# VectorE block transposes, one load of wo and a ScalarE store in a decode block with an adaptive LayerNorm

## The chip, the cores and the metric

The kernel runs on one core of one Trainium2 chip. The metric is the time of one execution on the device in microseconds (us). The profiled execution gives a span, from the first to the last instruction of the program; the run time is some 1.2 to 1.5 us longer than the span.

## The reference

One token for each of two sequences goes through a transformer block. A modulation vector is computed from `c`; attention reads a window of 1024 positions of a K and a V cache (32 heads of 192); a gated FFN follows.

```python
mod = (_silu(c) @ w_mod).reshape(c.shape[0], 6, 1, -1)
sa, ca, ga, sb, cb, gb = (mod[:, i] for i in range(6))
h = _layernorm(x) * (1 + ca) + sa            # x: [2, 1, 640]
x = x + ga * attention(h, k_cache, v_cache, wq, wo)   # wq 640 x 6144, wo 6144 x 640
h = _layernorm(x) * (1 + cb) + sb
x = x + gb * ((_gelu(h @ w_gate) * (h @ w_up)) @ w_down)  # F = 1536
```

There are two rows of activations and 76.88 MB of weights and cache, so the work is mostly to bring data in.

## The kernel before

All big operands go through one arena in SBUF. The sync engine issues the loads in a fixed order (w_mod, wq, K and V tiles, wo, gate, up, down), each as soon as the place it overwrites has been read. Small matmuls use four groups of columns of TensorE side by side, so a row of activations is kept as four pieces, on partitions 0 to 31, 32 to 63 and so on.

The normalised row `hrow` is turned to the contraction layout by matmuls with a selector (the same code serves LN1 and LN2):

```python
for j in range(KT):
    for i in range(NR):
        last = e.matmul(ps[32*i:32*i+32, BK_M, CT+2*j:CT+2*j+2], lhsT=hv[:, :, j],
                        rhs=selrow[:, i, :], ..., tile_position=(0, 32*i))
...
S.op("dve", lambda e: e.tensor_copy(out=dst_bf, in_=ps[:, BK_M, CT:CT+2*KT]...))
```

wo arrives in two loads, `WO_SPLIT = [(0, 39), (39, 9)]`; its matmuls write four partial rows, which `wo_rows` adds up. Before them, `keep_clock(9, "clock0")` runs nine filler matmuls, whose results nobody reads. Gate and up read the weights in runs of three columns:

```python
wk = wv[:, k, :].rearrange("p (m i r) -> p i m r", i=NR, r=FR)      # FR = 3
for i in range(NR):
    last = e.matmul(ps[32*i:32*i+B, bk, 0:FT]..., lhsT=h2T[:, k, :], rhs=wk[:, i, :, :], ...)
```

The gated row is turned by three matmuls and a copy (`a_T`), and w_down arrives in pieces of 8, 3 and 1 blocks, `WD_SPLIT = [(0, 8), (8, 3), (11, 1)]`. The last four matmuls, two VectorE operations and the store of 2.5 KB, issued by the sync engine, end the program.

## Time and profile before

| | before |
|---|---|
| run time, median | 185.97 us (185.87 to 185.97, 3 runs) |
| span of the profiled run | 184.9 us |
| bytes loaded | 76.88 MB, 416 GB/s over the span |
| TensorE / VectorE / ScalarE busy | 56% / 58% / 8% |
| last landing of weights / end of span | 182.05 / 184.9 us |

Busy shares say little here, since every compute engine idles much of the time.

### The profile page before, as it was taken

The page shows a single profiled execution, that of the slowest core. Times are in us where ns is not written, and L with a number is a line of the kernel's source. Part 1 is how long each engine was busy: PE and PEld are TensorE (multiplying, and loading weights), DVE is VectorE, ACT ScalarE, POOL GpSimd, SP SyncE. Part 2 cuts the span into 40 slices and gives each one's busy share as a digit, 9 for nine tenths or more (in the row PEclk, how much of TensorE's full clock was granted, in tenths as well). Part 3 has the DMA queues.
Part 4 walks back from the last instruction along what each step waited for, and adds up shares of the span by engine and source line. Part 5 has one row for each costly group of instructions (what it writes and reads, how often), then busy time and mean ns, then how long its engine had stood idle before and what let it go on. Part 6 is the DMA issues. An engine that isn't in the chain of part 4 may idle for free.

```text
span 184.9 us, 1610 instructions
## 1 busy us (share of the span) xinstructions
PE 104.3 (56%) x843; PEld 26.1 (14%) x552; DVE 106.8 (58%) x97; ACT 14.5 (8%) x28; POOL 6.7 (4%) x29
## 2 busy tenths in 40 slices
PE   0015400937666096662598667748663299866853
PEld 0011000020000000001360002400000266411211
DVE  6213000039996489965994999387995649302311
ACT  2032100060000000001000000100000100220410
POOL 7700000000000000000000000000000000000000
PEclk9999999996999759998599999987999669999999
DMA  9999998999897999999898989899999989899980
GB/s 349 433 495 425 425 425 362 429 425 495 367 511 340 511 404 447 457 394 479 374 479 365 500 351 500 383 468 436 425 450 394 491 367 486 378 388 435 419 365 28
DMA packets 2626, 76.97 MB, mean 416 GB/s; under 512 B 314, under 2 KB 444, under 8 KB 572
## 3 DMA queue, kind: packets, MB, share of 16 engines
q1 hardware_dynamic: 2604, 76.88, 96.9%
q8 instruction: 5, 0.08, 0.2%
q14 instruction: 1, 0.01, 0.0%
q10 hardware_dynamic: 16, 0.01, 0.0%
HBM read 76.88 MB, written 0.00 MB: 416 GB/s over the span
## 4 chain that ended last, share of the span: by engine, by line
DMA 57%; DVE 22%; PE 17%; ACT 1%; issue 1%; SPq 0%
DMA arena<-in_A_k_cache_dram 36%; DMA arena<-in_B_w_down_dram 14%; DVE arena L518 12%; DMA arena<-in_w_mod_dram 8%; PE ps L581 8%; DVE S_sb L537 6%; PE ps L530 5%; DVE Em L567 2%; PE ps L470 2%; DVE negm L547 1%; ACT E_sb L555 1%; PE ps L558 1%; DVE M L543 0%; PE ps L551 0%; SPq L287 0%
## 5 line engine op out<-in xcount | busy, mean ns | idle before, releaser
L530 PE MATMUL ps<-arena,ident_b 128*128 128x512 bf16 x192 | 50.7, 411 | 30.2 <-DVE arena L518 30.1
L518 DVE TENSOR_TENSOR arena<-arena,qbc 128x3072 bf16<-128x3072 bf16 x32 | 54.8, 1749 | 11.1 <-DMA arena<-in_A_k_cache_dram 11.1
L581 PE MATMUL ps<-arena,Em 128*64 128x384 bf16 x256 | 24.5, 357 | 5.6 <-DVE Em L567 5.6
L537 DVE TENSOR_REDUCE S_sb<-ps 128x32 f32<-128x1024 f32 x16 | 19.5, 1219 | 8.4 <-PE ps L530 8.4
L581 PEld LDWEIGHTS ps<-arena,Em 128*64 128x64 bf16 x256 | 15.4, 121 | 29.8 <-DVE Em L567 22.2
L567 DVE TENSOR_TENSOR Em<-E_sb,maskE 128x2048 bf16<-128x2048 bf16 x8 | 18.0, 2282 | 2.6 <-PE ps L581 2.6
L492 PE MATMUL ps<-arena,hT 128*2 128x512 bf16 x60 | 4.7, 485 | 11.7 <-DMA arena<-in_A_wq_dram 11.7
L502 DVE CAST qrow<-ps 128x512 bf16<-128x512 f32 x1 | 0.7, 693 | 15.6 <-PE ps L492 15.6
L545 PEld LDWEIGHTS ps<-ident_f,M 128*1 128x1 f32 x2 | 0.2, 80 | 61.5 <-DVE M L543 61.5
L555 ACT ACTIVATE E_sb<-S_sb,nbias 128x256 bf16<-128x256 f32 x2 | 1.0, 507 | 69.3 <-DVE nbias L553 69.3
L651 DVE COPY arena<-ps 128x320 f32<-128x320 f32 x1 | 0.5, 491 | 10.1 <-PE ps L643 10.1
L643 PE MATMUL ps<-arena,oT 128*2 128x320 bf16 x96 | 3.9, 299 | 2.4 <-DMA arena<-in_A_wo_dram 2.4
L588 ACT ACTIVATE On<-ps,rden 128x384 bf16<-128x384 f32 x2 | 1.2, 582 | 47.5 <-PE ps L581 47.5
L403 PE MATMUL ps<-ident_b,crow 2*128 2x2 bf16 x5 | 0.4, 177 | 7.9 <-POOL zsel L383 7.9
L678 PE MATMUL ps<-arena,h2T 128*2 128x384 bf16 x40 | 3.8, 455 | 1.7 <-DMA arena<-in_B_w_up_dram 1.4
L470 PE MATMUL ps<-arena,scT 128*17 128x480 bf16 x40 | 4.3, 597 | 0.5 <-DMA arena<-in_w_mod_dram 0.5
L415 PE MATMUL ps<-Em,ident_b 128*128 128x512 bf16 x17 | 4.2, 379 | 0.2 <-issue 0.2
L408 DVE CAST X<-xr 128x160 f32<-128x160 bf16 x1 | 0.2, 244 | 6.1 <-DMA xr<-in_A_x_dram 6.1
L687 DVE TENSOR_TENSOR aR<-ps,gl 128x384 bf16<-128x384 f32 x1 | 0.6, 558 | 5.4 <-PE ps L678 5.4
L424 PE MATMUL ps<-st,selstat 128*128 128x2 f32 x4 | 0.9, 298 | 4.9 <-ACT sqj L420 4.9
L478 DVE TENSOR_SCALAR opc<-modR 128x160 f32<-128x160 f32 x2 | 0.5, 245 | 5.1 <-ACT modR L475 5.1
L492 PEld LDWEIGHTS ps<-arena,hT 128*2 128x2 bf16 x20 | 0.6, 100 | 15.8 <-issue 15.8
(89 smaller groups left out, 52.6 us busy)
## 6 DMA issues: line engine op xcount, KB each, us to landing
arena<-in_A_v_cache_dram SPq DMA_DIRECT2D x4, 6144.0 KB, 27.2
arena<-in_A_k_cache_dram SPq DMA_DIRECT2D x3, 6144.0 KB, 36.0
arena<-in_A_wq_dram SPq DMA_DIRECT2D x1, 7680.0 KB, 31.3
arena<-in_A_wo_dram SPq DMA_DIRECT2D x1, 6240.0 KB, 27.0
arena<-in_A_k_cache_dram SPq DMA_DIRECT2D x2, 3072.0 KB, 42.7
arena<-in_w_mod_dram SPq DMA_DIRECT2D x1, 4800.0 KB, 14.0
arena<-in_B_w_gate_dram SPq DMA_DIRECT2D x1, 1920.0 KB, 20.7
arena<-in_B_w_up_dram SPq DMA_DIRECT2D x1, 1920.0 KB, 22.7
```

Of the source, the lines that this page charges most:

```text
L415: last = e.matmul(ps[:, BK_T, :], lhsT=ident_b[:, :], rhs=Em[:, 0, 0:512 // H, :].rearrange("p j h -> p (j h)"), start=True, stop=True)
L470: last = e.matmul(ps[32 * i:32 * i + RM, half, 0:MH].rearrange("p (m n) -> p m n", n=DR), lhsT=scT[:, k, :], rhs=wv[:, 3 * half:3 * half + ...
L492: last = e.matmul(ps[32 * i:32 * i + B, n, :], lhsT=hT[:, k, :], rhs=wv[:, kk, i, n * QW:(n + 1) * QW], start=(k == 0), stop=(k == KT - 1) ...
L518: S.op("dve", lambda e: e.tensor_tensor(out=kt, in0=kt, in1=qbc[:, b, :].unsqueeze(1).broadcast_to([P, JC, Dh]), op=ALU.mult), reads=[("qb ...
L530: last = e.matmul(o_ap, lhsT=ident_b[:, :], rhs=kt[:, :, t * GC:(t + 1) * GC], start=(t == 0), stop=(t == NCH - 1))
L537: S.op("dve", lambda e: e.tensor_reduce(out=S_sb[:, b, 2 * JC * pair:2 * JC * (pair + 1)], in_=ps[:, 2 * z:2 * z + 2, :].rearrange("p k (j ...
L547: S.op("dve", lambda e: e.tensor_reduce(out=negm[:, b, :].rearrange("p (h x) -> p h x", x=XQ), in_=ps[0:1, BK_T, 0:P].rearrange("p (h x) - ...
L555: S.op("act", lambda e: e.activation(out=E_sb[:, b, :], in_=S_sb[:, b, :], func=ACTF.Exp, scale=SCALE, bias=nbias[:, b:b + 1], accum_out=d ...
L567: S.op("dve", lambda e, z=z, j=j: e.tensor_tensor(out=Em[:, z, :, :], in0=E_sb[:, b, j:j + JE].unsqueeze(2).broadcast_to([P, JE, H]), in1= ...
L581: last = e.matmul(ps[64 * i:64 * i + 2 * H, BK_O, 0:ON], lhsT=Em[:, z, 2 * jp:2 * jp + 2, :].rearrange("p j h -> p (j h)"), rhs=view(it, l ...
L643: last = e.matmul(ps[32 * i:32 * i + B, bk, 0:w], lhsT=oT[:, t, :], rhs=wv[:, tl, lo:lo + w], start=(t < NR), stop=(t >= NT - NR), tile_po ...
L678: last = e.matmul(ps[32 * i:32 * i + B, bk, 0:FT].rearrange("p (m r) -> p m r", r=FR), lhsT=h2T[:, k, :], rhs=wk[:, i, :, :], start=(k == ...
```

## The change

The intent is to shorten the chain from the landing of wo to the end: no transposes through TensorE and PSUM, contiguous weight reads in gate and up, fewer loads, and a store issued by an engine other than the loading one. The diff, cut to its core:

```diff
-    WO_SPLIT = [(0, 39), (39, 9)]
+    WO_SPLIT = [(0, NT)]
 ...
-            S.op("pe", f, reads=["hrow", "selrow"], writes=[bank(BK_M)], name=tag + "_T")
-            S.op("dve", lambda e: e.tensor_copy(out=dst_bf[:, :, :], in_=ps[:, BK_M, ...
+            S.op("dve", lambda e: e.transpose(dst_bf[:, :, :], hrow[:, :].rearrange("p (m j) -> p j m", j=KT)),
+                 reads=["hrow"], writes=[tag + "_out"], name=tag + "_T")
 ...
-        keep_clock(9, "clock0")
+        keep_clock(31, "clock0")
 ...
-                        wk = wv[:, k, :].rearrange("p (m i r) -> p i m r", i=NR, r=FR)
-                            last = e.matmul(ps[32 * i:32 * i + B, bk, 0:FT]..., lhsT=h2T[:, k, :], rhs=wk[:, i, :, :], ...
+                            last = e.matmul(ps[32 * i:32 * i + RM, bk, 0:FT], lhsT=h2T[:, k, 0:RM], rhs=wv[:, k, i * FT:(i + 1) * FT], ...
 ...  (gelu and the product now read PSUM with a stride of 12 and write rows sorted for the transpose)
-        S.op("pe", a_T, reads=["aR", "selg"], writes=[bank(2)], name="aT_T")
-        S.op("dve", lambda e: e.tensor_copy(out=aT[:, :, 0:RM:RB]...
+        S.op("dve", lambda e: e.transpose(aT[:, :, :], aR[:, :].rearrange("p (r m) -> p r m", r=FC)), ...)
 ...
-        S.dma("sp", k_dma(out[:, 0, :]...
+        S.dma("act", k_dma(out[:, 0, :]...
```

The summing of wo in partial rows is in both kernels and its lines don't change.

More of the change, by code (lines that the diff above doesn't have):

```diff
@@ L149, in bass_adaLN_cond__sliding_block_cached__geglu_ffn__decode_kernel @@
     DD = Dh // NT
-    FR = 3
     FC = F // P
     assert B == 2 and D == KT * P and XQ * J == W and XQ * H == P and HB * NR == H and NT * P == NQ
-    assert DD * NT == Dh and DD * H == P and NR * FR == FC and FC * P == F and DR == KT * 32 and DD == XQ
+    assert DD * NT == Dh and DD * H == P and FC * P == F and DR == KT * 32 and DD == XQ
     SCALE = float(Dh) ** -0.5
@@ L203, in bass_adaLN_cond__sliding_block_cached__geglu_ffn__decode_kernel @@
         place[("wo", 0)] = (4 * HS, wo_n[0])
-        place[("wo", 1)] = (13 * HS, wo_n[1])
-        assert 4 * HS + wo_n[0] <= 9 * HS and wo_n[1] <= HS
+        assert wo_n[0] == 5 * HS
         o_g = 9 * HS
@@ L232, in bass_adaLN_cond__sliding_block_cached__geglu_ffn__decode_kernel @@
         selstat = sb("selstat", [P, P], F32)
-        selrow = sb("selrow", [P, NR, B], BF16)
         selq = sb("selq", [P, B, HB * SQW], BF16)
@@ L251, in bass_adaLN_cond__sliding_block_cached__geglu_ffn__decode_kernel @@
         hrow = sb("hrow", [P, DR], BF16)
-        hT = sb("hT", [P, KT, B], BF16)
-        h2T = sb("h2T", [P, KT, B], BF16)
+        hT = sb("hT", [P, KT, 32], BF16)
+        h2T = sb("h2T", [P, KT, 32], BF16)
         S_sb = sb("S_sb", [P, B, J], F32)
@@ L262, in bass_adaLN_cond__sliding_block_cached__geglu_ffn__decode_kernel @@
         selw = sb("selw", [P, RM], F32)
-        gl = sb("gl", [P, FT], F32)
+        assert FT <= B * J
+        gl = S_sb[:, :, :].rearrange("p b j -> p (b j)")[:, 0:FT]
         aR = sb("aR", [P, FT], BF16)
-        selg = sb("selg", [P, NR, B], BF16)
-        aT = sb("aT", [P, FC, RM], BF16)
+        aT = sb("aT", [P, FC, 32], BF16)
         fin = sb("fin", [P, DR], F32)
@@ L346, in bass_adaLN_cond__sliding_block_cached__geglu_ffn__decode_kernel @@
         S.op("pool", lambda e: e.memset(epsc[:, 1:2], EPS), reads=["epsc"], writes=["epsc"], name="epsc1")
-        for nm, t in (("scT", scT), ("aT", aT)):
+        for nm, t in (("scT", scT),):
             S.op("pool", lambda e, t=t: e.memset(t[:, :, :], 0.0), writes=[nm], name=nm + "0")
@@ L356, in bass_adaLN_cond__sliding_block_cached__geglu_ffn__decode_kernel @@
              reads=["ident_f"], writes=["ident_b"], name="ident_b")
-        S.op("pool", lambda e: e.affine_select(out=selrow[:, :, :], in_=ones_b[:, 0:1].unsqueeze(2).broadcast_to([P, NR, B]),
-                                                pattern=[[-32, NR], [-RB, B]],
-                                                compare_op=ALU.is_equal, fill=0.0, base=0, channel_multiplier=1),
-             reads=["ones_b"], writes=["selrow"], name="selrow")
-        S.op("pool", lambda e: e.affine_select(out=selg[:, :, :], in_=ones_b[:, 0:1].unsqueeze(2).broadcast_to([P, NR, B]),
-                                                pattern=[[-32, NR], [-1, B]],
-                                                compare_op=ALU.is_equal, fill=0.0, base=0, channel_multiplier=1),
-             reads=["ones_b"], writes=["selg"], name="selg")
         S.op("pool", lambda e: e.memset(selw[:, :], 0.0), writes=["selw"], name="selw0")
@@ L444, in ln_mod @@
                  reads=["lnt", "rstd", ("modR", s_idx // 3)], writes=["hrow"], name=tag + "_h")
-            def f(e):
-                last = None
-                hv = hrow[:, :].rearrange("p (m j) -> p m j", j=KT)
-                for j in range(KT):
-                    for i in range(NR):
-                        last = e.matmul(ps[32 * i:32 * i + 32, BK_M, CT + 2 * j:CT + 2 * j + 2], lhsT=hv[:, :, j], rhs=selrow[:, i, :],
-                                        start=(j == 0), stop=(j == KT - 1), skip_group_check=True, tile_position=(0, 32 * i))
-                return last
-            S.op("pe", f, reads=["hrow", "selrow"], writes=[bank(BK_M)], name=tag + "_T")
-            S.op("dve", lambda e: e.tensor_copy(out=dst_bf[:, :, :], in_=ps[:, BK_M, CT:CT + 2 * KT].rearrange("p (j b) -> p j b", b=B)),
-                 reads=[bank(BK_M)], writes=[tag + "_out"], name=tag + "_out")
+            S.op("dve", lambda e: e.transpose(dst_bf[:, :, :], hrow[:, :].rearrange("p (m j) -> p j m", j=KT)),
+                 reads=["hrow"], writes=[tag + "_out"], name=tag + "_T")
         ln_stats("ln1")
@@ L491, in f @@
                         for i in range(NR):
-                            last = e.matmul(ps[32 * i:32 * i + B, n, :], lhsT=hT[:, k, :], rhs=wv[:, kk, i, n * QW:(n + 1) * QW],
+                            last = e.matmul(ps[32 * i:32 * i + B, n, :], lhsT=hT[:, k, 0:RM:RB], rhs=wv[:, kk, i, n * QW:(n + 1) * QW],
                                             start=(k == 0), stop=(k == KT - 1), tile_position=(0, 32 * i))
@@ L675, in f @@
                     for k in range(k0, k0 + nk):
-                        wk = wv[:, k, :].rearrange("p (m i r) -> p i m r", i=NR, r=FR)
                         for i in range(NR):
-                            last = e.matmul(ps[32 * i:32 * i + B, bk, 0:FT].rearrange("p (m r) -> p m r", r=FR), lhsT=h2T[:, k, :],
-                                            rhs=wk[:, i, :, :], start=(k == 0), stop=(k == KT - 1), tile_position=(0, 32 * i))
+                            last = e.matmul(ps[32 * i:32 * i + RM, bk, 0:FT], lhsT=h2T[:, k, 0:RM], rhs=wv[:, k, i * FT:(i + 1) * FT],
+                                            start=(k == 0), stop=(k == KT - 1), tile_position=(0, 32 * i))
                     return last
@@ L683, in bass_adaLN_cond__sliding_block_cached__geglu_ffn__decode_kernel @@
         ffn_gu(0, wg_v, "gate", [(0, KT, ("wg", 0))])
-        S.op("act", lambda e: e.activation(out=gl[:, :], in_=ps[:, 0, 0:FT], func=ACTF.Gelu_apprx_tanh),
+        S.op("act", lambda e: e.activation(out=gl[:, :].rearrange("p (r m) -> p r m", r=FC), in_=ps[:, 0, 0:FT].rearrange("p (m r) -> p r m", r=FC), func=ACTF.Gelu_apprx_tanh),
              reads=[bank(0)], writes=["gl"], name="gelu")
         ffn_gu(1, wu_v, "up", [(k0, nk, ("wu", ci)) for ci, (k0, nk) in enumerate(WU_SPLIT)])
-        S.op("dve", lambda e: e.tensor_tensor(out=aR[:, :], in0=ps[:, 1, 0:FT], in1=gl[:, :], op=ALU.mult),
+        S.op("dve", lambda e: e.tensor_tensor(out=aR[:, :].rearrange("p (r m) -> p r m", r=FC), in0=ps[:, 1, 0:FT].rearrange("p (m r) -> p r m", r=FC),
+                                              in1=gl[:, :].rearrange("p (r m) -> p r m", r=FC), op=ALU.mult),
              reads=[bank(1), "gl"], writes=["aR"], name="geglu")
-        def a_T(e):
-            last = None
-            for r in range(FR):
-                last = e.matmul(ps[:, 2, NR * B * r:NR * B * (r + 1)], lhsT=aR[:, :].rearrange("p (m r) -> p m r", r=FR)[:, :, r],
-                                rhs=selg[:, :, :].rearrange("p i b -> p (i b)"), start=True, stop=True)
-            return last
-        S.op("pe", a_T, reads=["aR", "selg"], writes=[bank(2)], name="aT_T")
-        S.op("dve", lambda e: e.tensor_copy(out=aT[:, :, 0:RM:RB].rearrange("p (i r) b -> p i r b", r=FR),
-                                            in_=ps[:, 2, 0:FC * B].rearrange("p (r i b) -> p i r b", r=FR, i=NR)),
-             reads=[bank(2)], writes=["aT"], name="aT")
+        S.op("dve", lambda e: e.transpose(aT[:, :, :], aR[:, :].rearrange("p (r m) -> p r m", r=FC)), reads=["aR"], writes=["aT"], name="aT")
         for ci, (r0, nr) in enumerate(WD_SPLIT):
@@ L705, in f @@
                     for i in range(NR):
-                        last = e.matmul(ps[32 * i:32 * i + RM, BK_OT, CY:CY + DR], lhsT=aT[:, fc, :], rhs=wv[:, i, :],
+                        last = e.matmul(ps[32 * i:32 * i + RM, BK_OT, CY:CY + DR], lhsT=aT[:, fc, 0:RM], rhs=wv[:, i, :],
                                         start=(fc == WD_SPLIT[0][0]), stop=(fc == WD_SPLIT[-1][0]), tile_position=(0, 32 * i))
@@ L714, in bass_adaLN_cond__sliding_block_cached__geglu_ffn__decode_kernel @@
              reads=["fin", "X"], writes=["finb"], name="outR")
-        S.dma("sp", k_dma(out[:, 0, :].rearrange("b (i n) -> i b n", i=NR), finb[0:P:RB, :]),
+        S.dma("act", k_dma(out[:, 0, :].rearrange("b (i n) -> i b n", i=NR), finb[0:P:RB, :]),
               sem_out, reads=["finb"], name="st_out")
@@ L727, in bass_adaLN_cond__sliding_block_cached__geglu_ffn__decode_kernel @@
         body[entry:entry] = moved
-        S.emit("sp", nc.sync, tail=lambda e: e.wait_ge(sem_out, 16))
+        S.emit("sp", nc.sync)
         S.emit("pool", nc.gpsimd)
-        S.emit("act", nc.scalar)
+        S.emit("act", nc.scalar, tail=lambda e: e.wait_ge(sem_out, 16))
         S.emit("dve", nc.vector)
```

## The prediction

> **What bounds the kernel now.** I began with the page: the row of DMA activity in 40 slices, to see whether one resource is busy from end to end, and the count of moved bytes.
>
> ```profile
> DMA  9999998999897999999898989899999989899980
> ...
> HBM read 76.88 MB, written 0.00 MB: 416 GB/s over the span
> DMA 57%; DVE 22%; PE 17%; ACT 1%; issue 1%; SPq 0%
> ```
>
> The transfer engines never go quiet before the last slice, while PE and DVE are each busy under 60% of the span. So the program is a stream of 76.88 MB that begins at 0 and must end before the last weights can be used. The chain that ended last ends like this (start, duration, what):
>
> ```profile
> 155.58 26.07 DMA arena<-in_B_w_down_dram
> 181.65 0.04 issue
> 181.70 0.39 PE ps L706 x12
> 182.08 0.01 issue
> 182.09 0.28 PE ps L706 x4
> 182.37 0.02 issue
> 182.39 0.34 DVE fin L711
> 182.73 0.02 issue
> 182.75 0.33 DVE finb L713
> ```
>
> The last two pieces of the down projection wait for their weights, which land at about 181.65 and 182.08. From the last landing to the end of the 184.9 us span there are only 2.8 us: four matmuls, two VectorE operations and the store. The busy time of each engine by stretch shows how the stream ends (the columns are the stretch, its length, PE, PEld, DVE, ACT and POOL busy with counts, granted clock, DMA share, GB/s):
>
> ```profile
> 177.00:179.00 2.00, 1.55 (x20) 0.59 (x20) 0.00 (x0) 0.00 (x0) 0.00 (x0) 1.00 0.99 402
> 179.00:180.60 1.60, 0.60 (x7) 0.15 (x3) 0.76 (x2) 0.00 (x0) 0.00 (x0) 1.00 0.60 235
> 180.60:181.70 1.10, 0.74 (x33) 0.55 (x34) 0.00 (x0) 0.00 (x0) 0.00 (x0) 1.00 0.18 69
> ```
>
> All 16 transfer engines work until 179; then most are finished, and the last piece lands when the slowest one is. No compute instruction sets that moment. Finally the timeline of the part that the change touches:
>
> ```profile
> 164.80 2.89 PE L643 MATMUL ps<-arena,oT 128*2 128x320 bf16 x78 [1.78 <-DMA arena<-in_A_wo_dram]
> 168.27 0.98 PE L643 MATMUL ps<-arena,oT 128*2 128x320 bf16 x18 [0.58 <-DMA arena<-in_A_wo_dram]
> 173.45 0.37 PE L451 MATMUL ps<-selrow,hrow 128*32 128x2 bf16 x20 [0.26 <-DVE hrow L442]
> 174.09 1.91 PE L678 MATMUL ps<-arena,h2T 128*2 128x384 bf16 x20 [0.27 <-DVE h2T L455]
> 177.45 1.91 PE L678 MATMUL ps<-arena,h2T 128*2 128x384 bf16 x20 [1.45 <-DMA arena<-in_B_w_up_dram]
> 180.10 0.24 PE L693 MATMUL ps<-selg,aR 128*128 128x8 bf16 x3 [0.74 <-DVE aR L687]
> 180.65 0.73 PE L706 MATMUL ps<-arena,aT 128*17 128x160 bf16 x32 [0.31 <-DVE aT L697]
> 183.10 0.69 SPq L287 DMA_DIRECT2D out_dram<-finb  x1
> ```
>
> Here wo arrives in two parts (landing at 164.8 and 168.27), LN2 follows, gate and up run, then the first eight blocks of down. The gate matmuls wait for LN2, but the up matmuls wait for their own weights (177.45), so LN2 and gate have slack of 1.45 us today, and the down blocks then wait again for weights.
>
> **What the Trainium skill says.** (1) "VectorE: DVE Perf Modes", section "The three transpose paths": the VectorE transpose works on 32x32 blocks from SBUF to SBUF, 311 ns for 128x128 bf16. No such instruction is in this trace, so that figure is my basis. (2) "SBUF — State Buffer", section "Door 1: The DMA port swizzle", note on cachelines: a read that moves to a new 16-byte line for each access pays, with at least two accesses per line needed. The gate and up weights are read today in runs of three bf16 (6 bytes) at a pitch of 24 bytes. The trace agrees in direction: 20 gate matmuls take 1.91 us, so four side by side take 0.382 us for 384 columns, 0.99 ns a column; the wo matmuls, whose rows are contiguous, take 2.89/78 x 4 = 0.148 us for 320 columns, 0.46 ns a column. (3) "TensorE: Matmul & The Clock Gate", section "Part 1: The HAM clock gate (the "warmup" mystery)": about 3.4 us of idle halves the clock. The column of the granted clock reads 1.00 around the modulation matmuls at 14 us, yet twenty of 480 columns take 2.18 us, 0.91 ns a column after an idle time, twice wo's, so I believe the durations, not the column. It is why the filler matmuls rise from 9 to 31. (4) "DMA: Bandwidth & Descriptors", section "Issuing engines are not separate DMA queues": another issuing engine saves only the sequencer's issue time. In this trace the ACT issues of x and c took 0.61 and 0.54 us, the SP issue of the result 0.69.
>
> **The change, part by part.**
>
> LN1 transpose. Removed: 20 small matmuls (0.37 us) and a cast (0.17). Added: one VectorE transpose of 128x160, estimated at 0.311 + 32/0.96 ns = 0.34 us. The query matmuls that read it wait for wq until 32.2 us, while hT is ready at 18.7. Worth 0. The second modulation group no longer waits behind the transposes and ends some 2 us sooner, so a K load is issued at about 18.5 in place of 20.5; wq and two K tiles are queued before it, so the stream does not notice. Worth 0. The smaller GpSimd setup is done by 8.4 us anyway. Worth 0.
>
> wo in one load. The same 7680 KB are read. Its issue now also waits for the last reduction of the last K tile: 140.6 in place of 137.8 us, while the queue still holds two V tiles. Its landing stays at about 168.2, since the later part already landed last. But the 78 matmuls that ran from 164.8 now start only at 168.3, so 96 follow in a row: 96 x 0.0371 = 3.56 us, end 171.85 against 169.25. This part costs 2.6 us on the compute chain. The filler: 31 at some 0.22 us from 160.9 ends near 167.8, ahead of the landing, so it costs nothing and keeps the clock.
>
> LN2. From the end of wo to the end of hrow is 4.14 us today, unchanged: hrow ends at 171.85 + 4.14 = 176.0. Today h2T is there and gate starts 0.70 us after hrow; with a transpose of 0.34 us and its hand-over, some 0.4. Gate starts at 176.4 (today 174.09).
>
> Gate and up, read contiguously: at 0.46 ns a column, five groups of 384 take 5 x 0.178 = 0.89, with fill some 1.05 us. Gate ends 177.45, just as the up weights land (177.42); up ends 178.5, against 179.4 today. The gelu (0.49) is done at 178.0. This part gives back 0.86 us each.
>
> geglu stays near 0.56 us (reads at a pitch of 48 bytes from PSUM might add 0.1 to 0.3): 179.1. The transpose of 128x384 is 0.311 + 256/0.96 ns = 0.58 us; today three matmuls, a cast and hand-overs take 0.58 from 180.05 to 180.63. A wash. aT is ready at about 179.75, against 180.63 today.
>
> Down and end. The first eight blocks' weights land by about 180.5 (issue 155.09 + 25.4), the next at 181.65, the last at 182.08; so the gain of some 0.9 us is waited away. The operand could be as late as 181.05 (182.08 less 0.73 less 0.28) without loss. After that the four matmuls and two operations are as before, and the store's issue takes 0.6 on ACT in place of 0.69: -0.1 us. The receipt (about 1.0 us) stays.
>
> One more small term: wq, rows of 61,440 bytes like the merged wo, came in at 7.86 MB / 18.2 us = 432 GB/s, and the second wo part at 1.47 MB / 3.47 us = 425; over 18 us that is up to 0.2 us of stream, of which I count half at half belief. Sum: -0.1 - 0.05, so about 185.8 us.
>
> **The rivals.** (A) The compute chain overtakes the stream. If strided reading is not what slows gate and up, they keep 1.91 us: gate ends 178.35, up 180.25, aT is ready near 181.45, 0.4 us after the harmless limit: 186.4 us. For it: other matmuls after idle times are slow too. Against it: gate runs right after filler, up after 1.45 us of idle, and both take 1.91. If also wo ran at half clock, 3.5 us more: near 190. Against it: the filler reaches to the landing. (B) The stream itself gets shorter, by fewer and larger packets, and the slowest engine ends sooner: at most some 0.5 us, 185.3. Against it: the piece of 1280-byte rows, 160 KB, took 0.4 us, about 400 GB/s, so short rows cost little. (C) The store from ACT is slower, its queue having been unused since 2 us: up to +0.3, 186.2. For it: nothing that the profile shows.
>
> **Range and chances.** The end is tied to the landing of the last bytes, which no part moves, and the three runs of before lie within 0.1 us. B gives the low end with the store's gain, A's smaller form the high end: 185.2 to 186.4. Faster by 2% would be under 182.3 us, about where the last load lands: 1%. Slower by 2% would be over 189.7, which needs half clock and slow reads together: 1%.
>
> **What would show it.** Right: wo's 96 matmuls start at 168.3 and take about 3.6 us; gate and up take about 1.05 us each; the transposes 0.34 and 0.58 us; down's later blocks still wait for weights, landing at 181.65 and 182.08; issue on ACT near 0.6 us. Wrong: a last wait of down on aT in place of the weights, gate at 1.9 us, wo at 0.07 us or more a matmul, or a last landing moved by over 0.5 us.

## The result, and the profile after

| | before | after |
|---|---|---|
| run time, median | 185.98 us (185.87 to 186.16, 6 runs) | 186.12 us (186.03 to 186.40, 6 runs) |
| span of the profiled run | 184.9 us | 184.7 us |
| last landing of weights | 182.05 us | 181.95 us |
| instructions | 1610 | 1541 |

The ratio is 1.0008 with a 95% interval of 0.9995 to 1.0021: the same time. A ratio is the mean time of one kernel's fast runs over that of the other's of the same rounds, so it is not quite the ratio of the medians quoted. In the page of the changed kernel, the activity of the transfer engines, the bytes and the shares of the chain that ended last:

```profile
DMA  9999998999898989999898989899998999979990
...
HBM read 76.88 MB, written 0.00 MB: 416 GB/s over the span
DMA 57%; DVE 22%; PE 18%; ACT 1%; issue 1%; SPq 0%
```

The stream is as dense as before, with the same bytes. The end of the chain of waits of the changed kernel (start, duration, what):

```profile
156.83 24.71 DMA arena<-in_B_w_down_dram
181.55 0.04 issue
181.59 0.39 PE ps L676 x12
181.98 0.01 issue
181.99 0.28 PE ps L676 x4
182.27 0.02 issue
182.29 0.34 DVE fin L681
182.63 0.02 issue
182.65 0.32 DVE finb L683
```

The same waits end last: the two late pieces of w_down, now at 181.55 and about 181.95. The stretches at the end of the stream (columns as in the prediction):

```profile
179.00:180.60 1.60, 0.10 (x8) 0.13 (x12) 1.07 (x2) 0.00 (x0) 0.00 (x0) 1.00 0.59 221
180.60:181.70 1.10, 0.75 (x40) 0.54 (x40) 0.00 (x0) 0.00 (x0) 0.00 (x0) 1.00 0.15 56
```

The share of busy transfer engines falls to 0.59 and then 0.15, as before. And the timeline of the changed part:

```profile
162.39 6.64 PE L404 MATMUL ps<-Em,ident_b 128*128 128x512 bf16 x30
168.96 3.44 PE L623 MATMUL ps<-arena,oT 128*2 128x320 bf16 x96
176.60 0.35 DVE L435 STREAM_TRANSPOSE h2T<-hrow 128x160 bf16<-128x160 bf16 x1
177.01 1.80 PE L657 MATMUL ps<-arena,h2T 128*17 128x384 bf16 x40 [0.65 <-DVE h2T L435]
179.53 0.58 DVE L669 STREAM_TRANSPOSE aT<-aR 128x384 bf16<-128x384 bf16 x1
180.50 0.73 PE L676 MATMUL ps<-arena,aT 128*17 128x160 bf16 x32 [1.69 <-DMA arena<-in_B_w_down_dram]
183.01 0.60 ACTq L284 DMA_DIRECT2D out_dram<-finb  x1
```

wo starts four microseconds later than before (168.96 against 164.80) and runs without a break. Gate and up together take 1.80 us where they took 1.91 us each. The transposed activation is ready at 180.11; then TensorE waits for the first piece of w_down, which in the kernel before it met almost without a wait (0.31 us idle, ended by aT).

### The profile page after: what moved, and what is told of

The parts are those of the page before. It is cut to its first block, busy times and chain, and to the rows that moved or that the text cites. A ratio compares the mean times of both kernels' runs of the same rounds, so it can differ in the third digit from the quotient of the medians.

```text
span 184.7 us, 1541 instructions
## 1 busy us (share of the span) xinstructions
PE 107.9 (58%) x822; PEld 27.1 (15%) x509; DVE 106.8 (58%) x97; ACT 14.5 (8%) x28; POOL 6.1 (3%) x26
## 4 chain that ended last, share of the span: by engine, by line
DMA 57%; DVE 22%; PE 18%; ACT 1%; issue 1%; SPq 0%
DMA arena<-in_A_k_cache_dram 36%; DMA arena<-in_B_w_down_dram 13%; DVE arena L498 12%; PE ps L561 9%; DMA arena<-in_w_mod_dram 8%; DVE S_sb L517 6%; PE ps L510 5%; DVE Em L547 2%; PE ps L450 2%; DVE negm L527 1%; ACT E_sb L535 1%; PE ps L538 1%; PE ps L531 1%; DVE M L523 0%; SPq L284 0%
## 5 line engine op out<-in xcount | busy, mean ns | idle before, releaser
L510 PE MATMUL ps<-arena,ident_b 128*128 128x512 bf16 x192 | 49.4, 400 | 28.5 <-DVE arena L498 28.5
L561 PE MATMUL ps<-arena,Em 128*64 128x384 bf16 x256 | 27.1, 384 | 5.7 <-DVE Em L547 5.7
L561 PEld LDWEIGHTS ps<-arena,Em 128*64 128x64 bf16 x256 | 16.8, 130 | 31.0 <-DVE Em L547 22.0
L472 PE MATMUL ps<-arena,hT 128*2 128x512 bf16 x60 | 6.0, 585 | 14.5 <-DMA arena<-in_A_wq_dram 14.5
L404 PE MATMUL ps<-Em,ident_b 128*128 128x512 bf16 x39 | 8.9, 379 | 0.2 <-issue 0.2
L450 PE MATMUL ps<-arena,scT 128*17 128x480 bf16 x40 | 3.7, 542 | 0.5 <-DMA arena<-in_w_mod_dram 0.5
L623 PE MATMUL ps<-arena,oT 128*2 128x320 bf16 x96 | 3.4, 299 | 0.0
L479 ACT ACTIVATE qrow<-ps 128x512 bf16<-128x512 f32 x2 | 1.1, 594 | 19.9 <-PE ps L472 19.9
L525 PE MATMUL ps<-ident_f,M 128*1 128x128 f32 x2 | 0.5, 270 | 3.5 <-DVE M L523 3.5
L676 PE MATMUL ps<-arena,aT 128*17 128x160 bf16 x48 | 1.4, 234 | 2.1 <-DMA arena<-in_B_w_down_dram 2.0
```

What stands on the lines that cost most here:

```text
L404: last = e.matmul(ps[:, BK_T, :], lhsT=ident_b[:, :], rhs=Em[:, 0, 0:512 // H, :].rearrange("p j h -> p (j h)"), start=True, stop=True)
L450: last = e.matmul(ps[32 * i:32 * i + RM, half, 0:MH].rearrange("p (m n) -> p m n", n=DR), lhsT=scT[:, k, :], rhs=wv[:, 3 * half:3 * half + ...
L472: last = e.matmul(ps[32 * i:32 * i + B, n, :], lhsT=hT[:, k, 0:RM:RB], rhs=wv[:, kk, i, n * QW:(n + 1) * QW], start=(k == 0), stop=(k == K ...
L510: last = e.matmul(o_ap, lhsT=ident_b[:, :], rhs=kt[:, :, t * GC:(t + 1) * GC], start=(t == 0), stop=(t == NCH - 1))
L561: last = e.matmul(ps[64 * i:64 * i + 2 * H, BK_O, 0:ON], lhsT=Em[:, z, 2 * jp:2 * jp + 2, :].rearrange("p j h -> p (j h)"), rhs=view(it, l ...
L623: last = e.matmul(ps[32 * i:32 * i + B, bk, 0:w], lhsT=oT[:, t, :], rhs=wv[:, tl, lo:lo + w], start=(t < NR), stop=(t >= NT - NR), tile_po ...
```

## The experiments

Eleven kernels ran. All are correct except where the text says "wrong"; the ratio in each is to the kernel before in the same rounds.

### The store's issuer

Two runs tell the issuing engine apart from the rest: the changed kernel with the store on the sync engine (`a_sp`), and the kernel before with only the store moved (`b_act`).

```diff
# a_sp, against the changed kernel; b_act is the reverse edit of the kernel before
-        S.dma("act", k_dma(out[:, 0, :]...
+        S.dma("sp", k_dma(out[:, 0, :]...
-        S.emit("act", nc.scalar, tail=lambda e: e.wait_ge(sem_out, 16))
+        S.emit("act", nc.scalar)
-        S.emit("sp", nc.sync)
+        S.emit("sp", nc.sync, tail=lambda e: e.wait_ge(sem_out, 16))
```

> The changed kernel with its store issued by the sync engine again; nothing else differs. Theory S (the store from ScalarE is 0.1 us quicker inside the span, but lengthens the time outside the span by 0.2 us, since the gap between run time and span went from 1.21 to 1.43 us): issue back to 0.69 us, gap near 1.2 us, time about 185.95 us, so ratio to before about 1.000. Rival (the issuing engine makes no difference to the end, the +0.14 us is chance or comes from the other parts): about 186.1 us.

> The kernel before with only the store moved to ScalarE. Theory S: span shorter by 0.1 us, gap between run time and span near 1.4 us, time about 186.1 us (+0.1 to +0.2). Rival (only the sequencer's issue time is saved): 185.9 us, gap unchanged at 1.2.

Measured: `a_sp` 186.20 us (5 runs, ratio 1.0008, 0.9994 to 1.0021), `b_act` 186.10 us (5 runs, 1.0002, 0.9990 to 1.0015). Neither moved in run time, so theory S's forecasts of the time fall.

The two shifts that it named are there, though, when the spans of all runs are read and not those of the profiled runs alone. The mean span of `b_act` is 184.66 us, against 184.77 for the kernel before in the same rounds. The gap between run time and span is 1.37 to 1.53 us in all 43 runs of kernels with the store on ScalarE (mean 1.44 in the changed kernel, 1.40 in `b_act`). With the store on the sync engine it is 1.21 to 1.31 in the kernel before and in `b_short`, and 1.21 to 1.40 (mean 1.31) in `a_sp`. So some 0.1 us is saved inside the span and about as much lost outside it. Spans are on record to 0.1 us only, so single gaps say little and the means more. The edit moves the issue and the final wait for the receipt together; which of them lengthens the time outside is not shown.

In the traces the issue takes 0.60 (after) and 0.59 us (`b_act`) on ScalarE against 0.69 on the sync engine. From issue to the receipt of the last part it is 1.67 and 1.66 us on ScalarE and 1.72 in both kernels with the sync engine. The 0.14 us between the medians of the two kernels is within the scatter of the runs, which lie 0.3 us apart.

### wo in two loads again

```diff
# a_split, against the changed kernel; the lines that place the second load in the arena are left out
-    WO_SPLIT = [(0, NT)]
+    WO_SPLIT = [(0, 39), (39, 9)]
-        keep_clock(31, "clock0")
+        keep_clock(9, "clock0")
```

> The changed kernel with wo in two loads (39 and 9 blocks) and 9 filler matmuls, as before. Theory T1 (the landing of the last weights sets the end, the compute chain has slack): wo's matmuls end 2.5 to 3 us sooner, the transposed activation is ready at about 177.5 in place of 180.1 us, down still starts at about 180.4 when its weights land, time 186.1 us, unchanged. Rival T2 (the compute chain sets the end, the gains in gate and up were merely paid for by the later wo): about 183.5 us.

Measured: 186.14 us (4 runs, ratio 1.0005, 0.9992 to 1.0019), unchanged. wo's matmuls ended at 169.2 in place of 172.4, but part of my expectation was wrong. Two lines of its timeline:

```profile
173.75 0.99 PE L658 MATMUL ps<-arena,h2T 128*17 128x384 bf16 x20 [0.65 <-DVE h2T L436]
177.37 0.99 PE L658 MATMUL ps<-arena,h2T 128*17 128x384 bf16 x20 [2.62 <-DMA arena<-in_B_w_up_dram]
```

The up weights land at 177.3 in any case, so the activation was ready at 179.65, not 177.5, and rival T2's 183.5 us could not have come about either. The run shows that three microseconds saved at wo are lost at the next load, but it does not separate T1 from T2 as sharply as meant. The runs with a shorter stream do.

### A stream shorter by the up weights

Here the up projection reads the gate weights and w_up is never loaded; the result is wrong, and the compute instructions stay. The edit was made to the kernel before (`b_short`), to the changed kernel (`a_short`), and to `a_split` (`a_split_short`).

```diff
-        for i, (k0, nk) in enumerate(WU_SPLIT):
-            place[("wu", i)] = (o_u + k0 * F, nk * F)
-        ffn_gu(1, wu_v, "up", [(k0, nk, ("wu", ci)) for ci, (k0, nk) in enumerate(WU_SPLIT)])
+        ffn_gu(1, wg_v, "up", [(0, KT, ("wg", 0))])
```

> The kernel before, wrong on purpose: the up projection reads the gate weights and the up weights are not loaded, so the stream is 1.97 MB, some 4.6 us, shorter; the compute instructions stay. Theory T1 with a compute chain close behind the stream: the last weights land near 177.4, and the compute chain becomes the bound: gate 174.1 to 176.0, up to 177.9, product and transpose to 179.1, all 48 down matmuls to about 180.2 in place of 182.3, so 2.1 us shorter: 183.9 us. If the stream alone counted: 4.6 us shorter, 181.4. If the stream did not count: 186.0.

> The changed kernel with the same shortened stream, wrong on purpose. T1 with the compute chain behind: activation ready at 179.5 to 180.1, down to about 180.6 to 181.3, so 1.0 to 1.6 us shorter than the changed kernel: 184.5 to 185.1 us, that is slower than the shortened kernel before by 0.6 to 1.3 us, because wo in one load is now on the path. If the change's compute part was worth anything in itself: 183.9 or less.

> The changed kernel with wo in two loads and 9 filler matmuls, and the shortened stream, wrong on purpose. Gate would run 173.8 to 174.7, up to 175.6, activation ready near 176.9, before the last landing at 177.4: the stream is the bound again and the whole 4.6 us come out: 181.6 us. If the compute chain could not go faster than in the kernel before: 183.9 us.

| kernel | run time, median (4 runs each) | ratio to before | last landing | activation ready |
|---|---|---|---|---|
| before, shorter stream | 184.33 us | 0.9902 (0.9876 to 0.9928) | 177.20 | 178.72 |
| changed, shorter stream | 184.60 us | 0.9928 (0.9909 to 0.9947) | 177.19 | 179.30 |
| changed, wo in two loads, shorter stream | 181.94 us | 0.9788 (0.9756 to 0.9820) | 177.75 | 177.19 |

The down matmuls in these three, in the timelines of `b_short`, `a_short` and `a_split_short`:

```profile
178.76 1.01 PE L704 MATMUL ps<-arena,aT 128*17 128x160 bf16 x48 [0.30 <-DVE aT L695]
```

```profile
179.35 1.01 PE L674 MATMUL ps<-arena,aT 128*17 128x160 bf16 x48 [1.35 <-DVE aT L667]
```

```profile
177.24 1.01 PE L675 MATMUL ps<-arena,aT 128*17 128x160 bf16 x48 [1.35 <-DVE aT L668]
```

In all three, the 48 run in one go, and what they waited for last is the activation aT, not a load. (Landing and readiness are those of the one profiled run of each kernel, of 183.58, 184.25 and 182.13 us.) With the stream 4.8 us shorter, the kernel before wins only 1.6 us: its compute chain takes over as the bound. The changed kernel wins 1.5 us and is not faster than the kernel before, although its gate and up are quicker, because wo in one load holds its chain back. With wo in two loads 4.2 us come out. That is within 0.4 us of the 181.6 expected, but not for the reason given: the stream was not the bound again, since aT (177.19) still ended the last wait; the last landing, at 177.75, came 0.3 us before the last four matmuls started. Of the other two, `b_short` lies 0.4 us above its expected time and `a_short` inside its range; runs of one kernel spread by 0.6 to 1.3 us here.

So T1 holds as far as this: a shorter stream shortens the time until the compute chain ends last. The three traces also show what the change's parts are worth where compute binds. From the start of wo's last matmuls to the activation it takes 10.73 us in `b_short` (167.99 to 178.72) and 8.67 in `a_split_short` (168.52 to 177.19): transposes and contiguous reads are worth 2.1 us, of which gate and up alone make 1.9 (1.80 us against 3.68). wo in one load loses 2.5 us again: after the landing 96 matmuls remain (3.44 us) and not 18 (0.97). The medians differ by 2.4 and 2.7. In the real kernel both are hidden behind the stream.

### The reading pattern of gate and up

```diff
# a_strided, against the changed kernel: runs of three, each row group in its own block of 384 columns
-  rhs=wv[:, k, i * FT:(i + 1) * FT]
+  rhs=wv[:, k, i * FT:(i + 1) * FT].rearrange("p (m g r) -> p g m r", g=4, r=3)
   (gelu and the product read PSUM in the order that puts this right)
# a_interleaved, wrong on purpose: the columns of the kernel before
+  wk = wv[:, k, :].rearrange("p (m i r) -> p i m r", i=NR, r=3);  rhs=wk[:, i, :, :]
```

> The changed kernel whose gate and up matmuls read their weights again in runs of three at a pitch of twelve elements (the permuted columns are put right by the reads of PSUM in gelu and in the product). If the reading pattern is what made them slow: 1.9 us each in place of 0.9, activation ready near 182.1 us, which is 1.1 us past the harmless limit of about 181.0, so 187.2 us. If the clock made the difference and not the pattern: 0.9 us each, 186.1 us.

> The changed kernel with gate and up reading exactly the weight columns that the kernel before reads (runs of three, the four row groups side by side in the same 24 bytes), wrong on purpose. The run a_strided, with runs of three but each row group in its own block, took about 1.5 us for twenty matmuls, between 0.9 and 1.9. If the four groups reading neighbouring bytes makes the rest: 1.9 us each here; the activation is ready near 181.6, past the harmless limit of 181.0, and the time rises by 0.5 us to about 186.6. If the wider stationary operand (17 columns in place of 2) made the difference instead: 1.5 us each, 186.0 us.

The 40 gate and up matmuls in the timeline of `a_strided`, then of `a_interleaved`:

```profile
176.47 3.02 PE L657 MATMUL ps<-arena,h2T 128*17 128x384 bf16 x40 [0.65 <-DVE h2T L435]
```

```profile
176.17 3.63 PE L658 MATMUL ps<-arena,h2T 128*17 128x384 bf16 x40 [0.65 <-DVE h2T L435]
```

Against 1.80 us for contiguous reads, runs of three in separate blocks take 3.02 us, and runs of three in which the four groups read neighbouring bytes take 3.63. The pattern makes the difference, not the clock, but a third of it (0.61 of 1.83 us) comes from the four groups reading side by side, which my expectation for `a_strided` missed. The wider stationary operand is not the cause, since `a_interleaved` has it too and is about as slow as before. Why neighbouring reads are slower is not shown by these runs, nor that the short runs are slow because of 16-byte lines, as the prediction took it.

The times: `a_strided` 185.94 us (ratio 0.9999, 0.9985 to 1.0013), its activation ready at 180.77, just inside the limit of about 181.0; `a_interleaved` 186.30 us (1.0019, 1.0002 to 1.0036), ready at 181.10 and just past it. In `a_interleaved` all 48 down matmuls ran in one go after the activation, so compute ended last there. wo happened to start 0.5 and 0.8 us sooner in these two profiles than in the changed kernel's, so their activations came only 0.7 and 1.0 us later than its 180.11. Up to 1.8 us more in gate and up thus cost 0.2 us at most: most of it went into slack.

### The filler

```diff
# a_fill9, against the changed kernel
-        keep_clock(31, "clock0")
+        keep_clock(9, "clock0")
```

> The changed kernel with wo in one load but only 9 filler matmuls before it. If the filler is what keeps TensorE at full clock over the wait for wo: the 96 matmuls run at half clock, some 6.3 us in place of 3.44, the activation is ready some 3 us later, near 182, and the time rises by about 1 us to 187.2. If the clock did not fall in the wait, or wo's later end had slack enough: 186.1 us.

```profile
168.17 5.49 PE L623 MATMUL ps<-arena,oT 128*2 128x320 bf16 x96 [5.41 <-DMA arena<-in_A_wo_dram]
```

After 5.4 us of idle, wo's 96 matmuls took 5.49 us in place of 3.44 (timeline of `a_fill9`): some 64 of them at 267 ns for each four side by side, the rest at 136, as all in the changed kernel; so less than the 6.3 that I expected. The activation was ready at 181.4 and the time rose to 186.62 us (4 runs, ratio 1.0029, 1.0005 to 1.0053). All 48 down matmuls then ran in one go after the activation, so compute ended last in this profile. What the filler buys in run time, 0.5 us between the medians, is not clear of noise: the two ratios' intervals overlap.

### What makes the last landing late

In both kernels most transfer engines finish two microseconds before the slowest. Each load reports 16 completions, as many as the core has transfer engines, and I read each as the part of one engine. The packed trace has their times, and those of instruction fetches; no view of the profile lists them, so they were read from it directly. For the last load of w_down (1280 bytes a partition), in us:

```
before         179.93 179.99 180.00 180.03 180.04 180.05 180.06 180.27 180.28 180.62 180.93 181.43 181.64 181.71 181.81 182.05
after          179.95 179.96 179.97 179.99 180.00 180.03 180.04 180.13 180.16 180.19 180.39 181.19 181.45 181.47 181.82 181.95
a_pool512      179.94 179.95 180.02 180.05 180.08 180.13 180.52 180.75 180.81 181.31 181.38 181.41 181.55 181.61 182.08 183.10
a_pool         180.52 180.53 180.54 180.55 180.65 180.67 180.68 181.24 181.56 181.75 181.79 181.86 182.17 182.20 182.27 185.24
```

In the kernel after, five completions are over 0.7 us behind the other eleven. Going back through its loads, the number of such late completions rises one at a time: none in wq (31.5 to 32.1), one in the second K tile (47.74, the others by 46.72), two in the load that lands at 91, three in the one that lands at 106, and five in wo (168), after two more fetches. In the same trace the fetches of program instructions, 16 KB each and about 1.0 us long, start at 43.1, 98.8, 152.0, 166.1 and 179.4, with one of 8 KB at 89.6. Each late completion comes after a fetch; only the last fetch, after most data had landed, adds none. An engine that is slow from the start would be late from the first load on. In the kernel before, the fetches come at other times, 36.0, 89.4, 97.1, 134.6 and 162.5, and the late parts go with them: the first is already in its first K tile (40.62, the others by 39.43), where the changed kernel has none. This suggests that a fetch runs on one transfer engine and holds up the loads queued on it. To test it, GpSimd, idle after 8 us, was given extra instructions that touch nothing else:

```diff
# a_pool, against the changed kernel (a_pool512: range(512))
+        extra = sb("extra", [1, 1024], BF16)
+        def many(e):
+            for z in range(1024):
+                last = e.memset(extra[:, z:z + 1], 0.0)
+            return last
+        S.op("pool", many, writes=["extra"], name="extra")
```

> The changed kernel with 1024 one-element memsets added to GpSimd, which is otherwise idle from 8 us on; they touch nothing else. Theory F: each 16 KB fetch of instructions (5 in this kernel, about 1.0 us each in the trace) holds up one of the 16 transfer engines, and the engines so held up are the late ones whose landing sets the end. Then 64 KB more of instructions make 4 more fetches, and the last landing, 181.95 now, comes 0.3 to 1.2 us later: 186.4 to 187.3 us. If fetches cost the stream nothing: 186.1 us.

> Half as many extra GpSimd instructions as in a_pool, which made eight more fetches of 8 KB, and in which one of 16 landings came 3 us after the other fifteen. If all these fetches fall on one transfer engine and each holds it up by about 0.5 us: four more fetches, the last landing at about 183.0 in place of 181.95, time about 187.1 us. If it was the GpSimd work itself that slowed the stream, through a shared port or otherwise: half of the 4.0 us, 188.1 us, with all 16 landings later, not one.

Measured: `a_pool` 190.15 us (4 runs, ratio 1.0221, 1.0189 to 1.0253), `a_pool512` 186.97 us (4 runs, 1.0051, 1.0036 to 1.0067). The queues of the changed kernel, then of `a_pool` (packets, MB, share):

```profile
q14 instruction: 1, 0.01, 0.0%
```

```profile
q14 instruction: 9, 0.07, 0.1%
```

Eight more fetches of 8 KB moved the last landing by 3.3 us, to 185.24, which is 3 us after the other fifteen; those came 0.5 to 1.6 us later than in the changed kernel. Two stretches of `a_pool`:

```profile
182.00:183.00 1.00, 0.00 (x0) 0.00 (x0) 0.96 (x2) 0.00 (x0) 0.00 (x0) 1.00 0.07 31
183.00:185.20 2.20, 1.04 (x44) 0.74 (x44) 0.03 (x1) 0.00 (x0) 0.00 (x0) 1.00 0.05 19
```

The share of 0.05 to 0.07 is one engine of 16 (0.0625), so for over two microseconds one engine alone finishes its part while the core waits.

`a_pool512`, with four such fetches more, moved the last landing by 1.15 us, to 183.10 where 183.0 was expected. Half a microsecond a fetch is too little, though. Of wq's 16 parts in `a_pool512`, fifteen landed from 31.33 to 32.44 and one, after the four fetches (12.3 to 29.1), at 34.79: 3.15 us behind the median of the others, 0.8 us a fetch. At the end only what that part lags beyond the late parts of the changed kernel counts.

The rival, that GpSimd's work itself slows the stream, falls: that work ran until 28.9 us in `a_pool512`, and yet fifteen parts of wq came as in the changed kernel (31.50 to 32.11); at the end the six earliest lie within 0.1 us of the changed kernel's. Why some of the middle ones came up to 1.1 us later is open.

For `a_pool` I had expected four fetches of 16 KB on different engines; they were eight of 8 KB, whose delay fell on one part, and the delay was 3.3 us, not 1.2. That the first five fetches of the two main kernels (four of 16 KB and that of 8 KB), on different engines, cause their late completions is what the order of events says; no run took them away, so this part is argued and not shown. The trace does not say whose instructions they fetch. Those of 16 KB are probably TensorE's: in both kernels they come after about 210, 470, 720, 1000 and 1260 of its 1350 to 1410 instructions.

No run points to a version that clearly beats both kernels: the fastest of the correct ones, `a_strided`, is at 0.9999.

## Why the prediction was right

It said 185.8 us, range 185.2 to 186.4, the same within 2%; measured were 186.12 us.

- **The stream sets the end.** Right. The late pieces of w_down end the last waits at 181.55 and 181.95 (predicted 181.65 and 182.08), and the runs with a shorter stream show that the end moves with it until the compute chain takes over.
- **LN1 and setup worth 0.** Right. The second modulation group ended 2.8 us sooner, not 2: following the first without a gap, the 40 matmuls took 3.65 us in all, the last few at twice the speed of the rest (203 ns for four side by side against 400). The K load issued at 17.71 in place of 20.52 found a full queue.
- **wo in one load.** Right in kind: landing 168.25 (said 168.2), 3.44 us of matmuls (said 3.56). "So it costs nothing" of the filler failed in this profile: the attention matmuls before it ended 1.3 us later than in the profile before, so the filler ran to 169.0 and held wo up by 0.7 us. In `a_sp`, `a_short` and `a_interleaved` wo started at 168.1, so this varies from run to run; the slack absorbed it.
- **LN2.** Right: 0.35 us for the transpose (said 0.34), gate 0.44 us after hrow (said 0.4).
- **Gate and up.** Right in mechanism: 1.80 us for both in a row, and 0.99 each where they run apart in `a_split` (said 1.05 each). The pattern has a second component, the neighbouring reads, which the prediction did not have.
- **Product and transpose.** 0.56 us, so the strided PSUM reads cost nothing visible, and 0.58 us, both as said. Ready at 180.11 (said 179.75): the filler's 0.7 us, less what gate and up gave back by running in a row.
- **The store, -0.1 us.** Wrong in run time: the issue is 0.1 us shorter and so is the span, but the time outside the span, which the prediction did not count, is some 0.13 us longer.
- **Merged packets, -0.05 us.** Not seen: wo as a whole landed at 168.25 against 168.23 in two parts.
- **Rivals.** A is what `a_fill9` and `a_interleaved` bring about on purpose, with 0.2 to 0.5 us; in the change itself it did not happen. The sum behind its harmless limit, 182.08 less 0.73 less 0.28, is some 0.25 us too strict: all 48 down matmuls in one go, the last four among them, take 1.01 us. B did not happen. C is there in small, outside the span, and the shorter span makes up for it.

The 0.3 us between forecast and median are these two small credits (0.15), which did not come in run time, and the scatter of runs. That the number still fell well inside the range is due to the main point, that no part moves the last landing.

## What to carry to other kernels

When a stream of loads ends the program, ask of every compute saving which load it will wait for next; a saving before a load that lands later is worth nothing, however real it is. A stream cut short on purpose, with the compute kept, shows in one run how close the compute chain is behind it and what its parts would be worth. Look at the last landing by its parts as well as by its average: one late transfer engine sets it, and added instructions, even on an idle engine, can be what makes it late. And before a theory about a tenth of a microsecond is dropped, compare the spans of all runs and not of the profiled ones alone.

## What the Trainium skill lacked or had wrong

- "Runtime: NRT & Kernel Launch", section "Instruction fetch mechanics", calls the cost of crossing a block of instructions "one DMA tail-bump, mostly hidden". In this kernel, bound by loads, it is not hidden: eight extra fetches of 8 KB for GpSimd moved one of 16 landings by 3.3 us and the run time by 4.0 us (`a_pool`), and four by 1.15 us (`a_pool512`). That page gives 16 KB as the block; the fetches added with GpSimd's instructions came in packets of 8 KB here.
- "DMA: Bandwidth & Descriptors" has no word on the effect of such fetches on loads that share a transfer engine: in both kernels most of the 16 parts of the last load have landed by 180.4, the last only at about 182.
- "SBUF — State Buffer", note on cachelines, lets one expect slow short runs (3.02 us against 1.80 contiguous), but has no word on column groups that work side by side and read neighbouring bytes: 3.63 us with runs of the same length.
- No page tells what the issuer of the last store does outside the span: with ScalarE in place of the sync engine the gap between run time and span was 1.40 us in the mean (`b_act`) where the kernel before had 1.27 in the same rounds.
